# Clustered attention and two feed-forward layers on one core: two heads by plain loads, a gate, and a new order of the first slots

## The chip, the cores and the metric

One Trainium2 chip, one of its cores. The metric is the device time of one execution in microseconds (us). The core's engines are TensorE (PE; PEld is its weight load), VectorE (DVE), ScalarE (ACT), GpSimd (POOL) and SyncE (SP). SP, ACT and POOL can issue DMA transfers; each works through its own instructions in order, and a DMA whose condition is not met holds up what stands behind it on the same engine.

## The reference

Inputs: q, k, v of 2 batches x 8 heads x 768 positions x 64, and 16 centroids of 64 per head. A query may look at a key only if both have the same nearest centroid:

```
q_assign = argmax(q_n . c_n);  k_assign = argmax(k_n . c_n)      # per head, 16 clusters
scores = q @ k^T / 8, and -1e9 where q_assign != k_assign
attn = exp(scores - rowmax) / (rowsum + 1e-9);   o = attn @ v
x = o as [1536, 512]
x = (silu(x @ w_gate) * (x @ w_val)) @ w_out                      # d_ff 1536
p = domain_probs / rowsum                                         # 4 experts
out = sum over e of p[:, e] * (relu(x @ w1[e]) @ w2[e])           # d_ff 1024
```

## The kernel before

Everything runs on one core in two parts, `attention()` and `moe()`. The order of instructions on each engine is the order in which the program writes them. Products use float32r operands in two parts: a high part (the value rounded by a cast) and a low part (the value less its high part).

**Operands of a head.** There are 16 heads g (8 per batch). In memory `qk[b, h]` holds q and k of a head transposed, 128 rows: the 64 features twice, then q|k, then 768 positions. `t1` (128 x 2 x 768) is to hold, for q (index 0), the high part in rows 0 to 63 and the low part in rows 64 to 127, and for k (index 1) the low part in rows 0 to 63 and the high part in rows 64 to 127. `t2` (80 x 2 x 768) holds the high parts in rows 0 to 63 and 16 cluster rows in 64 to 79: one-hot for q, and 0 or -2^60 for k. `load_qk(g)` lets POOL issue casting DMA loads into t1 and t2 and lets SP load the two plain halves that the low parts are made from (`raw`); `rest_qk` (line 211) subtracts, on DVE for heads 0 and 1, on POOL for the others. Each head thus is read twice over from memory, 1.5 MB in all. `load_v` and `rest_v` do the like for v.

**Cluster steps.** `cluster(g)` is a generator that is advanced step by step: six matmuls for q, six for k (line 246), ACT's copy `sc`, DVE's add, maximum, comparison, tie-breaking product and maximum, one-hot `oh` (lines 255 to 264), six transposes to `pt` on TensorE, and the copies of `pt` into t2 (for head 0 one on ACT and one on DVE, lines 273 and 275; for others four half copies on ACT, lines 283 and 285). `pc` and `pt` live in single PSUM banks, `ps_c`, and `ps_v` for some heads.

**Slots.** 96 score tiles n (128 queries x 768 keys; six per head) are worked on in slots. `LEAD` is 5: slot s computes the scores of tile s+5 (S, lines 303 and 304), its negated maximum (M, line 309, DVE) and the exponential of tile s+4 (E, line 321, ACT with its accumulator read), and transposes two blocks of earlier tiles (line 327), casts them (ACT, line 332), makes low parts (DVE, line 346) and multiplies with v (lines 357 to 363). The letters of `ORDER = "ESTLAtVMlvZB"` give the sequence in a slot; A, Z and B run the side work that `at(slot, "a"|"z"|"b")` and `steps` have put there. A table of offsets per head (CL, CL1, CL2) says at which slots, counted from 6g, its cluster steps run; `load_qk(g)` for g > 3 runs at slot 6g-23, `rest_qk` at 6g-22 and 6g-20. The slots from -22 to -6 hold side work only, from -5 to -1 also scores. `warm(n)` issues n matmuls on zeros (line 451) as filler.

**Opening.** SP loads centroids, identity, the halves of head 0, wt and probs; POOL casts heads 0, 1, 2. `consts_setup` normalizes the centroids (DVE, ACT), transposes them on TensorE and writes `cT` in two parts. Then heads 1 to 3 and v are loaded, and `cluster(0)` runs.

**Second part.** `moe()` works through chunks of weights; TensorE multiplies, ACT and DVE finish the tiles and split the next weights (`w_steps`), whose pieces come by SP (`w_load`, two buffers). `probs_setup` makes the expert factors `pn`.

Of the kernel before, what the change touches and what calls it, by code (L numbers as in the profile page):

```python
# [7 lines left out]
F32 = mybir.dt.float32  # L8
# [10 lines left out]
NCL = 16  # L19
NT = B * S  # L20
# [15 lines left out]
def tile_cluster_attention_moe(ctx, tc, qk, vt, cent, consts, wm1, wm2, probs, out):  # L36
# [137 lines left out]
    def attention():  # L174
        with ExitStack() as ax:
# [14 lines left out]
            ops = {}  # L190

            def load_qk(g):
# [7 lines left out]
                if g == 0:  # L200
                    for j in range(2):
                        G.dma_start(out=t1[:, j], in_=src[:, j])
                else:
                    G.dma_start(out=t1, in_=src)
                G.dma_start(out=t2[0:64], in_=src[0:64])
# [21 lines left out]
            oh_t = [clp.tile([128, NQ, 2, 32], BF16, name=f"oh{h}") for h in range(2)]  # L227
            for h in range(2):
                V.memset(oh_t[h], 0.0)

            def cluster(g):
# [5 lines left out]
                ohn = oh[:, :, :, :NCL]  # L237
                pc = (ps_v if g in (1, 2) else ps_c).tile([128, N, 2, NCL], F32, tag="v" if g in (1, 2) else "c", name="pc")
                sc = clp.tile([128, N, NCL], F32, tag="sc", name="sc", bufs=2)
# [32 lines left out]
                if g == 0:  # L272
                    A.copy(out=t2[64:80, 0], in_=pt[0:16])
                    yield
                    V.tensor_scalar(out=t2[64:80, 1], in0=pt[32:48], scalar1=1.0, scalar2=BIG, op0=ALU.subtract, op1=ALU.mult)  # L275
# [168 lines left out]
            zeros = clp.tile([128, 384], BF16, name="zeros")  # L444
            V.memset(zeros, 0.0)

            def warm(n):
# [4 lines left out]

            consts_load(clp, ("cr", "ident"))
            load_qk(0)
            consts_load(clp, ("wt", "pr"))
            setup, rest = consts_setup(clp, ps_c), rest_qk(0, V)
            for gen in (setup, setup, rest):
                next(gen)
            for gen in (setup, rest):
                next(gen, None)  # L460
            load_qk(1)
            load_qk(2)
            load_v(0)
            load_qk(3)
            head, rest = cluster(0), rest_qk(1, V)
            for i, gen in enumerate((head,) * 10 + (rest, head, rest)):
                if i == 2:
                    warm(6)
                next(gen)
                if i == 8:  # L470
                    warm(6)
            for i in range(5):
                at(i - 4, "b", lambda: warm(3))
# [7 lines left out]
            CL1 = ("-10b", "-10z", "-9a", "-9b", "-9b", "-8a", "-8a", "-8b", "-7a", "-7b", "-7b", "-7z", "-7z")  # L481
            CL2 = ("-13z", "-13z", "-12a", "-12b", "-12b", "-12z", "-11a", "-10a", "-9b", "-9b", "-8b", "-7b", "-7z")
            for g in range(NH):
                c = 6 * g
                if g > 3:
                    at(c - 23, "z", lambda g=g: load_qk(g))
                if g > 1:
                    steps(c, ("-22b", "-20b"), lazy(rest_qk, g, G))
                if g:
                    steps(c, {1: CL1, 2: CL2}.get(g, CL), lazy(cluster, g))  # L490
                    at(c - 8, "z", lambda g=g: load_v(g))
                at(c - 4, "z", lambda g=g: rest_v(g))
# [66 lines left out]

    def consts_load(clp, names):  # L560
        src = {"cr": cent.rearrange("h c d -> (h c) d"), "ident": consts[:, 0:128],
               "wt": consts[:, 128:128 + NCL], "pr": probs}
        for n in names:
            ct[n] = ident if n == "ident" else clp.tile(list(src[n].shape), F32, name=n)
            SY.dma_start(out=ct[n], in_=src[n])

    def consts_setup(clp, ps_c):
        for n, w in (("sq", D), ("ss", 1), ("s1", 1), ("s2", 1), ("cn", 2 * D), ("prs", NT // 128)):
            ct[n] = clp.tile([128, w], F32, name=n)
# [18 lines left out]
        A.copy(out=cT[:, :, 0, :], in_=psv)  # L588
        V.tensor_tensor(out=cT[:, :, 1, :], in0=psv, in1=cT[:, :, 0, :].bitcast(F32), op=ALU.subtract)
        V.tensor_copy(out=identb, in_=ident)  # L590
        V.tensor_copy(out=wtie, in_=ct["wt"])
        V.memset(zero1, 0.0)
        A.activation(out=s2, in_=zero1, func=ACTF.Exp)

    def probs_setup():
        pr = ct["pr"]
        prs = ct["prs"].rearrange("p (t o) -> p t o", o=1)
        V.tensor_reduce(out=prs, in_=pr, axis=AX.X, op=ALU.add)
# [4 lines left out]
    def moe():  # L603
# [295 lines left out]
```

## Time and profile before

| | us |
|---|---|
| median of 3 runs | 1090.57 |
| lowest, highest | 1088.77, 1091.58 |
| span of the profiled execution | 1086.7 |
| TensorE busy in it | 1051.0 |
| DVE, ACT, POOL busy | 715.4, 465.0, 180.7 |

The span runs from the first to the last instruction that the profiler recorded; of the profiled execution's own time the profile gives no more than that, and the runs' times lie 2.1 to 4.9 us above it. Attention takes about the first 290 us, the second part the rest. A busy TensorE is not TensorE at its peak: matmuls are pipelined and their ends are modelled. An engine's time of waiting matters only where the engine that bounds the stage waits too.

### The profile page before, as it was taken

What the parts mean: (1) busy time and instruction counts of PE and PEld (TensorE: products, weight loads), DVE (VectorE), ACT (ScalarE), POOL (GpSimd) and SP (SyncE); (2) the same over time, 40 slices, a digit from 0 to 9 for tenths busy, and PEclk for the clock granted to TensorE, in tenths of its full rate; (3) what the DMA queues carried; (4) which work ended last, traced back from release to release, by engine and by line L of the source; (5) the groups of instructions that cost most, each with busy time, mean ns of one, the idle gap of its engine ahead of it and who ended that gap; (6) DMA issues with size and microseconds to landing.
All of it is one profiled execution on the core that took longest, in us unless ns stands there. A gap on an engine that the chain in (4) does not pass through costs nothing.

```text
span 1086.7 us, 13698 instructions
## 1 busy us (share of the span) xinstructions
PE 1051.0 (97%) x5178; PEld 871.6 (80%) x5178; DVE 715.4 (66%) x1243; ACT 465.0 (43%) x930; POOL 180.7 (17%) x182
## 2 busy tenths in 40 slices
PE   4899999999999999999999999999999999999998
PEld 2788778778788888888888888888888888888887
DVE  4799999898566655646658565655555665555564
ACT  1688888889554224414425222233322223333121
POOL 2526664542100000000101111111011111100100
PEclk9899999999999999999999999999999999999999
DMA  9866677551122212211200101111101011110103
GB/s 204 181 149 160 149 188 168 140 116 35 31 87 68 78 49 68 78 59 59 78 20 21 39 20 39 39 39 39 39 20 32 27 39 39 39 40 22 37 1 116
DMA packets 34801, 77.54 MB, mean 71 GB/s; under 512 B 12432, under 2 KB 17008, under 8 KB 34736
## 3 DMA queue, kind: packets, MB, share of 16 engines
q1 hardware_dynamic: 22560, 55.70, 18.3%
q0 software_dynamic: 12176, 20.97, 9.1%
q8 instruction: 40, 0.66, 0.3%
q14 instruction: 25, 0.20, 0.1%
HBM read 69.34 MB, written 3.19 MB: 67 GB/s over the span
## 4 chain that ended last, share of the span: by engine, by line
PE 88%; DVE 7%; DMA 2%; ACT 1%; issue 1%; SPq 0%; ACTq 0%; DVEq 0%
PE pd L834 24%; PE pb L163 17%; PE pa L704 12%; PE pd L801 9%; PE pa L163 9%; PE ps L327 5%; PE ps L303 2%; PE pb L704 2%; PE ps L304 2%; DVE junk L309 2%; DMA raw<-in_qk 2%; DVE lo L346 2%; PE pv L357 2%; PE pv L362 1%; PE pc L246 1%; PE pv L363 1%
## 5 line engine op out<-in xcount | busy, mean ns | idle before, releaser
L841 DVE SCALAR_TENSOR_TENSOR acc<-pd,pn,acc 128x512 f32<-128x512 f32 (+1 forms) x181 | 133.9, 746 | 89.6 <-PE pd L834 89.5
L834 PE MATMUL pd<-wdl,hh 128*128 128x512 f32 (+1 forms) x386 | 149.7, 388 | 0.0
L834 PE MATMUL pd<-wdh,hh 128*128 128x512 f32 (+1 forms) x386 | 149.7, 388 | 0.0
L834 PE MATMUL pd<-wdh,hl 128*128 128x512 f32 (+1 forms) x386 | 149.7, 388 | 0.0
L712 ACT COPY snap<-pa 128x512 f32<-128x512 f32 x48 | 28.2, 588 | 265.2 <-PE pa L704 265.2
L134 POOL TENSOR_TENSOR ws<-wraw 128x256 f32<-128x256 f32 x16 | 12.3, 772 | 671.8 <-DMA wraw<-in_wm 485.4
L163 PE MATMUL pb<-xh,wuh 128*128 128x512 f32 x264 | 102.7, 389 | 0.0
L163 PE MATMUL pb<-xl,wuh 128*128 128x512 f32 x264 | 102.7, 389 | 0.0
L163 PE MATMUL pb<-xh,wul 128*128 128x512 f32 x264 | 102.7, 389 | 0.0
L309 DVE CUSTOM_DVE_ANT_1 junk<-ps,zero 128x768 bf16<-128x768 f32 x96 | 91.0, 948 | 14.1 <-PE ps L304 13.0
L327 PE MATMUL ps<-ident,P 128*128 128x128 f32 x576 | 87.6, 279 | 12.4 <-DVE lo L346 10.2
L321 ACT ACTIVATE P<-ps,nm 128x768 f32<-128x768 f32 x96 | 87.0, 906 | 16.1 <-DVE nm L309 14.5
L327 PEld LDWEIGHTS ps<-ident,P 128*128 128x128 f32 x576 | 67.0, 141 | 26.8 <-DVE lo L346 17.3
L834 PEld LDWEIGHTS pd<-wdl,hh 128*128 128x128 f32 x386 | 72.5, 188 | 15.0
L834 PEld LDWEIGHTS pd<-wdh,hh 128*128 128x128 f32 x386 | 72.5, 188 | 14.9
L834 PEld LDWEIGHTS pd<-wdh,hl 128*128 128x128 f32 x386 | 72.5, 188 | 14.9
L346 DVE TENSOR_TENSOR lo<-ps,hi 128x384 fp32r<-128x384 f32 x128 | 67.5, 550 | 8.4 <-ACT hi L332 8.1
L303 PE MATMUL ps<-t 80*128 80x384 f32 x192 | 70.0, 365 | 1.6 <-DVE t L275 1.1
L304 PE MATMUL ps<-t 128*128 128x384 f32 x192 | 65.7, 342 | 0.0
L211 POOL TENSOR_TENSOR t<-raw,t 64x768 fp32r<-64x768 f32 x28 | 51.3, 1833 | 82.1 <-DMA raw<-in_qk 59.4
L332 ACT CAST hi<-ps 128x384 fp32r<-128x384 f32 x128 | 56.0, 482 | 19.1 <-PE ps L327 18.6
L717 ACT ACTIVATE hh<-sg 128x512 fp32r<-128x512 f32 x48 | 30.3, 632 | 72.3 <-DVE sg L724 72.3
(166 smaller groups left out, 2317.2 us busy)
## 6 DMA issues: line engine op xcount, KB each, us to landing
wraw<-in_wm SPq DMA_DIRECT2D x68, 512.0 KB, 3.8
t<-in_qk POOLq DMA_DIRECT2D x15, 768.0 KB, 5.7
t<-in_qk POOLq DMA_DIRECT2D x18, 384.0 KB, 6.7
raw<-in_qk SPq DMA_DIRECT2D x32, 192.0 KB, 6.5
x<-x SPq DMA_DIRECT2D x21, 192.0 KB, 5.9
R<-rd SPq DMA_DIRECT2D x16, 192.0 KB, 3.3
out<-acc SPq DMA_DIRECT2D x11, 256.0 KB, 2.0
vs<-in_vt POOLq DMA_DIRECT2D x16, 128.0 KB, 3.9
```

Of the source, the lines that this page charges most:

```text
L163: T.matmul(out=ps, lhsT=w[:, o:o + 128], rhs=x, start=(k == 0 and m == 0), stop=(k == 3 and m == 2))
L303: T.matmul(out=ps, lhsT=t2[:, 0, qs], rhs=t2[:, 1, ks], start=True, stop=False)
L304: T.matmul(out=ps, lhsT=t1[:, 0, qs], rhs=t1[:, 1, ks], start=False, stop=True)
L309: V.tensor_tensor_reduce(out=junk.rearrange("p (c n) -> p c n", c=2), in0=S_t[n][:, :, :384], in1=zero1.rearrange("p (o n) -> p o n", o=1) ...
L321: A.activation(out=P_t[n].rearrange("p (c n) -> p c n", c=2), in_=S_t.pop(n)[:, :, :384], func=ACTF.Exp, scale=0.125, bias=nm_t.pop(n), ac ...
L327: T.transpose(ps[:, i * 128:(i + 1) * 128], P_t[3 * u + i][:, j * 128:(j + 1) * 128], ident)
L332: A.copy(out=hi, in_=ps)
L346: V.tensor_tensor(out=lo, in0=ps, in1=hi.bitcast(F32), op=ALU.subtract)
L704: T.matmul(out=ps, lhsT=w[:, o:o + 128], rhs=r, start=first and i == 0 and m == 0, stop=i == 1 and m == 2, skip_group_check=not first)
L801: T.matmul(out=ps, lhsT=w[:, o:o + 128], rhs=x[:, f, sl], start=(n == 0), stop=(n == len(terms) - 1))
L834: T.matmul(out=ps, lhsT=x[:, f, ts_], rhs=w[:, f * DM + cs.start:f * DM + cs.stop], start=(f == 0 and m == 0), stop=(f == FC - 1 and m == 2))
L841: V.scalar_tensor_tensor(out=y, in0=ps, scalar=pe, in1=y, op0=ALU.mult, op1=ALU.add)
```

## The change

- Heads 0 and 1 (`load_raw`): SP loads q and k as they are, both copies of the features, into tiles of the pool of the exponentials (tag "P"). The high parts come by copies on the chip: `hi_raw` into t1 on ACT, `hi_t2` into t2 on DVE for head 0 and on ACT for head 1; `low_raw` subtracts on DVE. The four cast loads and four half loads of these heads are gone.
- Identity and wt are loaded from ACT's queue. `gate`: ACT copies one column of head 0's k into it, POOL overwrites it after; all POOL DMA issues of later heads and of v stand behind that on POOL.
- The opening is written out anew, with fillers of 11, 3, 5 and 8 matmuls, and ends with the first cluster step of head 1. The slots start at -5 instead of -22; head 1's remaining cluster steps run in slots -4 to 0, head 2's in 0 to 5 (`pc` now in `ps_c`), head 3's in 6 to 11, head 4's in 8 to 17. Loads of heads 3 and 4 are issued at slots -3 and 2. Filler triples run in slots -5 to -1 (before -4 to 0).
- Head 0's last operand is made in four halves, three on ACT and one on DVE.
- probs are loaded and `probs_setup` runs in the second part, after the first chunk's up products. The first two weight loads are issued at slot 9 instead of -2. The `zeros` memset stands ahead of those of `oh`, `zero1` is set with them.

```diff
+            def load_raw(g):
+                src = qk[g // H, g % H]
+                raw = [pp.tile([128, S], F32, tag="P", name="rawqk") for _ in range(2)]
...
+                for j in range(2):
+                    SY.dma_start(out=raw[j], in_=src[:, j])
+            def hi_raw(g, j, copy):
+                copy(out=ops[g]["t1"][:, j], in_=ops[g]["raw"][j])
+            def low_raw(g, j):
+                r = slice(64, 128) if j == 0 else slice(0, 64)
+                t = ops[g]["t1"][r, j]
+                V.tensor_tensor(out=t, in0=ops[g]["raw"][j][r], in1=t.bitcast(F32), op=ALU.subtract)
+            def hi_t2(g, j, copy):
+                copy(out=ops[g]["t2"][0:64, j], in_=ops[g]["raw"][j][0:64])
...
-                pc = (ps_v if g in (1, 2) else ps_c).tile([128, N, 2, NCL], F32, ...)
+                pc = (ps_v if g == 1 else ps_c).tile([128, N, 2, NCL], F32, ...)
...
-            consts_load(clp, ("cr", "ident"))
-            load_qk(0)
-            consts_load(clp, ("wt", "pr"))
...
+            consts_load(clp, SY, ("cr",))
+            load_raw(0)
+            consts_load(clp, A, ("ident", "wt"))
+            load_raw(1)
+            setup, head = consts_setup(clp, ps_c), cluster(0)
+            warm(11)
+            next(setup)
+            next(setup)
+            hi_raw(0, 0, A.copy)
+            next(setup)
+            low_raw(0, 0)
+            warm(3)
+            next(head)
+            hi_raw(0, 1, A.copy)
+            A.copy(out=gate, in_=ops[0]["raw"][1][:, 0:1])
+            G.memset(gate, 0.0)
+            low_raw(0, 1)
+            next(head)
+            warm(5)
+            next(setup, None)
+            load_v(0)
+            load_qk(2)
+            for j in range(2):
+                hi_t2(0, j, V.tensor_copy)
+            next(head)
+            for j in range(2):
+                hi_raw(1, j, A.copy)
+            for _ in range(5):
+                next(head)
+            warm(8)
+            low_raw(1, 0)
+            next(head)
+            next(head)
+            low_raw(1, 1)
+            for j in range(2):
+                hi_t2(1, j, A.copy)
+            head = cluster(1)
+            next(head)
...
-                steps(12 * (p + 1), ("1a", "2b", "2z"), recip(p))
+                steps(12 * (p + 1), ("1a", "2z", "2b"), recip(p))
...
+            CL1 = ("-4a", "-4z", "-3a", "-3a", "-3z", "-2a", "-2z", "-1a", "-1z", "-1b", "0z", "0b")
+            CL2 = ("-12z", "-12b", "-11a", "-11z", "-11b", "-10z", "-10b", "-9a", "-9b", "-9b", "-8z", "-7z", "-7b")
+            CL4 = ("-16a", "-16z", "-16b", "-15a", "-15z", "-14a", "-12a", "-9a", "-9b", "-9b", "-8z", "-7z", "-7b")
+            steps(0, CL1, head)
+            LQ = {3: -3, 4: 2}
+            RQ = {2: ("-13z", "-13b"), 3: ("-15b", "-13b"), 4: ("-19b", "-17b")}
...
-            at(-3, "z", probs_setup)
             for _ in range(2):
-                at(-2, "z", w_load)
+                at(9, "z", w_load)
...
-            for slot in range(-22, NS):
+            for slot in range(-LEAD, NS):
```

## Rows read from the trace of the kernel before

**Rows 1.** The page, part 1: busy us (share of the span) xinstructions.
```profile
PE 1051.0 (97%) x5178; PEld 871.6 (80%) x5178; DVE 715.4 (66%) x1243; ACT 465.0 (43%) x930; POOL 180.7 (17%) x182
```

**Rows 2.** Busy us by stage; last columns: granted clock, DMA share, GB/s.
```profile
0.00:24.29 24.29, 8.22 (x31) 4.92 (x32) 8.81 (x27) 4.34 (x7) 6.02 (x14) 1.00 1.17 196
24.29:42.39 18.10, 14.76 (x82) 12.52 (x82) 11.04 (x26) 8.33 (x19) 10.01 (x9) 0.81 1.02 212
42.39:73.66 31.27, 30.58 (x207) 25.68 (x205) 28.79 (x61) 25.54 (x59) 12.84 (x13) 1.00 0.54 117
73.66:277.00 203.34, 192.88 (x1293) 163.79 (x1293) 185.47 (x386) 175.63 (x399) 101.75 (x83) 1.00 0.60 141
277.00:1086.70 809.70, 804.55 (x3574) 664.65 (x3572) 481.27 (x746) 251.19 (x448) 50.09 (x65) 1.00 0.14 45
```

**Rows 3.** TensorE in order of time: start, us, instruction [idle before <-releaser]; line 303.
```profile
24.29 0.45 PE L303 MATMUL ps<-t 80*128 80x384 f32 x1 [1.11 <-DVE t L275]
...
42.39 0.48 PE L303 MATMUL ps<-t 80*128 80x384 f32 x1
...
275.94 0.34 PE L303 MATMUL ps<-t 80*128 80x384 f32 x1
```

**Rows 4.** The chain of waits, opening: start, us, what.
```profile
4.73 19.97 DMA raw<-in_qk
```

**Rows 5.** DVE in order of time, 0 to 32 us.
```profile
8.24 0.96 DVE L211 TENSOR_TENSOR t<-raw,t 64x768 fp32r<-64x768 f32 x1 [3.26 <-DMA raw<-in_qk]
...
15.09 0.17 DVE L591 CAST wtie<-wt 128x16 bf16<-128x16 f32 x1 [5.44 <-DMA wt<-in_consts]
...
18.04 0.36 DVE L255 TENSOR_TENSOR sc<-pc,sc 128x192 f32<-128x192 f32 x1 [1.91 <-ACT sc L253]
...
19.89 0.36 DVE L264 TENSOR_TENSOR oh<-eq,mw 128x192 bf16<-128x192 bf16 x1
...
22.30 0.96 DVE L211 TENSOR_TENSOR t<-raw,t 64x768 fp32r<-64x768 f32 x1 [2.05 <-DMA raw<-in_qk]
...
29.65 0.20 DVE L598 TENSOR_REDUCE prs<-pr 128x12 f32<-128x48 f32 x1
...
31.10 0.43 DVE L601 TENSOR_TENSOR pn<-pr,prs 128x48 f32<-128x48 f32 x1
```

**Rows 6.** The table by stage again, for the first 6 us.
```profile
0.00:4.50 4.50, 0.00 (x0) 0.00 (x0) 2.01 (x11) 1.49 (x2) 3.46 (x10) 1.00 0.51 100
4.50:6.00 1.50, 0.47 (x1) 0.18 (x1) 0.45 (x3) 0.44 (x2) 1.50 (x3) 1.00 1.32 281
```

**Rows 7.** ACT's groups up to 60 us: xcount | busy us, mean ns | idle before.
```profile
L321 ACT ACTIVATE P<-ps,nm 128x768 f32<-128x768 f32 x12 | 10.9, 907 | 11.1 <-DVE nm L309 10.9
L332 ACT CAST hi<-ps 128x384 fp32r<-128x384 f32 x12 | 5.4, 482 | 4.1 <-PE ps L327 4.1
L321 ACT ACTIVATION_READ_ACCUMULATOR P<-ps,nm 128x1 f32 x12 | 2.4, 198 | 0.0
...
L574 ACT ACT_TABLE_LOAD x1 | 1.3, 1283 | 0.7 <-PEq L887 0.7
```

**Rows 8.** TensorE in order of time, 17 to 27 us: fillers and cluster matmuls.
```profile
17.49 2.10 PE L451 MATMUL warm<-zeros 128*128 128x384 bf16 x6
...
25.82 0.73 PE L246 MATMUL pc<-cT,t 128*128 128x32 f32 x6
26.41 0.66 PE L451 MATMUL warm<-zeros 128*128 128x384 bf16 x3
```

**Rows 9.** The table by stage, 34.4 to 38.4 us.
```profile
34.40:38.40 4.00, 3.95 (x20) 3.48 (x21) 0.87 (x2) 3.44 (x8) 3.50 (x3) 0.50 1.01 314
```

**Rows 10.** POOL, then DVE, in order of time, 27 to 47 us.
```profile
27.06 3.71 POOL L211 TENSOR_TENSOR t<-raw,t 64x768 fp32r<-64x768 f32 x2 [15.78 <-DMA raw<-in_qk]
...
45.60 1.82 POOL L211 TENSOR_TENSOR t<-raw,t 64x768 fp32r<-64x768 f32 x1 [2.73 <-issue]
...
45.84 1.80 DVE L264 TENSOR_TENSOR oh<-eq,mw 128x192 bf16<-128x192 bf16 x1
```

More of the change, by code (lines that the diff above doesn't have):

```diff
@@ L190, in attention @@
             ops = {}
+            def load_raw(g):
+                src = qk[g // H, g % H]
+                raw = [pp.tile([128, S], F32, tag="P", name="rawqk") for _ in range(2)]
+                ops[g] = {"t1": qkp.tile([128, 2, S], F32R, tag="t1", name="t1", bufs=4),
+                          "t2": qkp.tile([80, 2, S], F32R, tag="t2", name="t2", bufs=4), "raw": raw}
+                for j in range(2):
[8 more added lines that the diff above has]
+                copy(out=ops[g]["t2"][0:64, j], in_=ops[g]["raw"][j][0:64])
             def load_qk(g):
@@ L199, in load_qk @@
                 SY.dma_start(out=raw[0:64], in_=src[0:64, 1])
[L200 to L204, printed above, removed]
+                G.dma_start(out=t1, in_=src)
                 G.dma_start(out=t2[0:64], in_=src[0:64])
@@ L227, in attention @@
             oh_t = [clp.tile([128, NQ, 2, 32], BF16, name=f"oh{h}") for h in range(2)]
-            for h in range(2):
-                V.memset(oh_t[h], 0.0)
             def cluster(g):
@@ L237, in cluster @@
                 ohn = oh[:, :, :, :NCL]
-                pc = (ps_v if g in (1, 2) else ps_c).tile([128, N, 2, NCL], F32, tag="v" if g in (1, 2) else "c", name="pc")
+                pc = (ps_v if g == 1 else ps_c).tile([128, N, 2, NCL], F32, tag="v" if g == 1 else "c", name="pc")
                 sc = clp.tile([128, N, NCL], F32, tag="sc", name="sc", bufs=2)
@@ L272, in cluster @@
                 if g == 0:
-                    A.copy(out=t2[64:80, 0], in_=pt[0:16])
-                    yield
-                    V.tensor_scalar(out=t2[64:80, 1], in0=pt[32:48], scalar1=1.0, scalar2=BIG, op0=ALU.subtract, op1=ALU.mult)
+                    hs = [slice(i * 384, (i + 1) * 384) for i in range(2)]
+                    A.activation(out=t2[64:80, 1, hs[0]], in_=pt[32:48, hs[0]], func=ACTF.Copy, scale=BIG, bias=-BIG)
+                    V.tensor_scalar(out=t2[64:80, 1, hs[1]], in0=pt[32:48, hs[1]], scalar1=1.0, scalar2=BIG, op0=ALU.subtract, op1=ALU.mult)
+                    for i in range(2):
+                        A.copy(out=t2[64:80, 0, hs[i]], in_=pt[0:16, hs[i]])
                     yield
@@ L445, in attention @@
             V.memset(zeros, 0.0)
+            for h in range(2):
+                V.memset(oh_t[h], 0.0)
+            V.memset(zero1, 0.0)
             def warm(n):
@@ L451, in warm @@
                     T.matmul(out=ps, lhsT=zeros[:, 0:128], rhs=zeros, start=True, stop=True)
-            consts_load(clp, ("cr", "ident"))
-            load_qk(0)
-            consts_load(clp, ("wt", "pr"))
[L456 to L461, printed above, removed]
-            load_qk(2)
[L463 to L471, printed above, removed]
+            gate = clp.tile([128, 1], F32, name="gate")
+            consts_load(clp, SY, ("cr",))
[19 more added lines that the diff above has]
+            load_v(0)
+            load_qk(2)
+            for j in range(2):
[14 more added lines that the diff above has]
+            next(head)
             for i in range(5):
-                at(i - 4, "b", lambda: warm(3))
+                at(i - 5, "b", lambda: warm(3))
             for i in range(4):
@@ L563, in consts_load @@
         for n in names:
-            ct[n] = ident if n == "ident" else clp.tile(list(src[n].shape), F32, name=n)
-            SY.dma_start(out=ct[n], in_=src[n])
+            ct[n] = ident if n == "ident" else pool.tile(list(src[n].shape), F32, name=n)
+            eng.dma_start(out=ct[n], in_=src[n])
     def consts_setup(clp, ps_c):
-        for n, w in (("sq", D), ("ss", 1), ("s1", 1), ("s2", 1), ("cn", 2 * D), ("prs", NT // 128)):
+        for n, w in (("sq", D), ("ss", 1), ("s1", 1), ("s2", 1), ("cn", 2 * D)):
             ct[n] = clp.tile([128, w], F32, name=n)
@@ L589, in consts_setup, with probs_setup @@
         V.tensor_tensor(out=cT[:, :, 1, :], in0=psv, in1=cT[:, :, 0, :].bitcast(F32), op=ALU.subtract)
+        yield
         V.tensor_copy(out=identb, in_=ident)
         V.tensor_copy(out=wtie, in_=ct["wt"])
-        V.memset(zero1, 0.0)
         A.activation(out=s2, in_=zero1, func=ACTF.Exp)
-    def probs_setup():
-        pr = ct["pr"]
-        prs = ct["prs"].rearrange("p (t o) -> p t o", o=1)
+    def probs_setup(pr, prs_t):
+        prs = prs_t.rearrange("p (t o) -> p t o", o=1)
         V.tensor_reduce(out=prs, in_=pr, axis=AX.X, op=ALU.add)
@@ L612, in moe @@
         acc2 = acc.rearrange("p (t n) -> p t n", n=DM)
+        consts_load(ap_, SY, ("pr",))
+        prs = ap_.tile([128, NT // 128], F32, name="prs")
         side = {"work": iter(()), "x": iter(()), "steps": 0, "calls": 0}
@@ L852, in moe @@
                 up(k)
+                if i == 0:
+                    probs_setup(ct["pr"], prs)
                 if k[1] % 2:
```

12 lines of the change are left out of this document (5 added, 7 removed).

## The prediction

> **What bounds the kernel now.** I read the page's busy line first: TensorE works in 97% of 1086.7 us [rows 1], so time can be won only where it stands idle or slow. The table by stage says where: up to 24.29 us it works 8.22 us, from there to 42.39 us 14.76 of 18.10 at a mean clock of 0.81, then 30.58 of 31.27, 192.88 of 203.34, and 804.55 of the last 809.70 [rows 2]. I name the steps of the attention part by their score matmuls of line 303: S0 opens slot -5 at 24.29, S6 (the first of head 1) opens slot 1 at 42.39, S95 comes at 275.94 [rows 3]: from S6 on a slot takes (275.94-42.39)/89 = 2.62 us. The change touches what lies ahead of S6 and the slots just after it, so the question is when S6 comes.
>
> The chain of waits shows the opening as one DMA wait of 19.97 us for halves of q and k ("raw") [rows 4]. The DVE timeline has the single waits behind it: the first subtract of line 211 starts at 8.24 after 3.26 us without its half; the cast of wt waits 5.44 us for a small load that stood behind others, and as DVE works in order, head 0's second subtract comes only after it, at 15.2; the first subtract of head 1 waits 2.05 us more, to 22.30 [rows 5], and head 0's last operand, line 275, stands behind that on DVE; S0 waits for it [rows 3].
>
> Own time against the median: of the profiled execution the page gives the span, 1086.7 us; the three runs lie 2.1 to 4.9 us above that, their median 3.9. What moves S6 moves both, so I subtract from both.
>
> **Head 0's data.** Before, the DMA engines carry head 0's halves and cast loads mixed with those of heads 1 and 2. They moved 0.45 MB in the first 4.5 us (100 GB/s) and 0.42 MB in the next 1.5 (281 GB/s) [rows 6]. After, SP's queue holds the centroids (0.03 MB), then q and k of head 0 (0.39 MB each), then head 1; identity and wt (0.07 MB) go by ACT's queue, and POOL's cast loads stand behind the gate. At the old pace the first operand is complete when 0.49 MB have come, at 4.7, the second at 0.89 MB, at 6.1; I take 4.8 and 6.3, and 7.9 and 9.5 for head 1. Bounds for the second: 5.5, if 281 GB/s hold from 2.7 us on; 8.2, if it lands no sooner than the half that freed DVE at 8.24 [rows 5].
>
> **Head 0's chain to S0.** Copies from SBUF on ACT and DVE are new. ACT's 128x768 lies between 0.91 (line 321, as many columns) and 0.96 (two casts of 384); I take 0.91. DVE's 64x768 lies between a half and the whole of the 0.95 of line 211; I take 0.95, the nearest row [rows 5, 7].
> ACT: first copy 4.8 to 5.7, cT 0.3 to 6.0, second copy 6.3 to 7.2, gate, table load of 1.28 [rows 7] and exp to 8.9. DVE: the rest of cT to 6.3, two subtracts to 8.2, two small casts to 8.6, two copies to 10.5. TensorE: twelve cluster matmuls from 7.3 to 9.3 (0.73 us for six at 26 us, up to twice that at half the clock [rows 8]). ACT's sc copy to 9.7. DVE's seven steps from add to one-hot took 18.04 to 20.25, 2.2 us [rows 5]: 10.5 to 12.7. In TensorE's order 13 fillers stand ahead of the transposes: 2.9 us at 0.22 or 4.6 at 0.35, the two rates of line 451 [rows 8], to 12.2 or 13.9. Transposes under 1 us, then three half copies of 0.48 on ACT [rows 7] (the fourth, on DVE, beside them). S0: 14.7 to 16.3, taken as 15.2, 9.1 us earlier. With the operands at their bounds: 14.4 to 17.5.
>
> **S0 to S6.** Before, 18.1 us. TensorE runs at granted 0.50 (the 1.2 GHz level) from 34.4 to 38.4 [rows 9], after an idle stretch that was head 1's chain: its raw, then the four steps of probs_setup, from 29.65 to 31.53 on DVE, ahead of head 1's add [rows 5]. Probs_setup now runs in the second part, beside TensorE at 99% and DVE at 59% [rows 2]: nothing there, 1.9 us if that cover were gone. What is late next is ACT: two copies for head 1 1.8, five exp with their accumulator read 5.5, sc 0.3, four half copies 1.9, two transposed casts of slot 0 1.0 [rows 7]: 10.5 us. S0 itself, the first max and the joints between ACT and DVE come on top; I take 12 to the last half copy. Then the twelve cluster matmuls of head 2, put at slot 0 ahead of S6 and in the PSUM bank that head 1's half copies free last: 1.5 us [rows 8], of which I count 1.2. S6 = 15.2 + 13.2 = 28.4 instead of 42.39: 14.0 earlier. Bounds of this stretch 11 and 16 us: S6 at 25.4 to 33.5.
>
> **DVE beside POOL.** Head 2's two POOL subtracts fall at about 18 to 23 us, beside head 1's DVE steps. At 45.84 a one-hot step took 1.80 us beside a POOL subtract begun at 45.60; undisturbed it took 0.36 [rows 5, 10]. Bounds: 0 to 2 x 1.5 us. I take 0, since between those DVE steps stand maxima that read PSUM and ACT is the later engine. The Trainium skill, "SBUF — State Buffer", section "Who interferes with whom", speaks against the change here: a DVE instruction with two SBUF inputs and a POOL instruction that reads SBUF shut each other out for a whole instruction. The row agrees; by the rule the time would be 3 us later, 1080.
>
> **After S6.** Heads 3 and 4 begin their cluster steps later and end by the slots that need them, so slots 0 to 5 hold less DVE work and slots 6 to 17 more; from S6 on there are six cluster matmuls more than before, 0.6 us. The weight loads at slot 9 have three slots, 7.9 us, to land; if they didn't, ACT would stand for the rest, under 2 us. "2b" and "2z" only change places in a list (z runs before b in each slot): nothing. The memsets only change places. The load of probs waits on SP for memory of the first part; behind it stand weight loads, covered by two pieces in flight; at most 2 us.
>
> **Sum:** -14.0 + 0.6 = -13.4: span 1073.3, median 1077.2; I say 1077.
>
> **Rivals.** (A) Smaller gain, 1084: the DMA engines are shared more than I count (only POOL is gated; SP sends v and raw of heads 2 and 3 without a wait), S0 comes 2 us later, and slots -5 to -1 run at the 1.2 GHz level, where four score matmuls and three fillers take 2.4 us instead of 1.4: 5 us more. 1077 + 7 = 1084. For it: the clock fell in this very stretch [rows 9]. Against it: fillers stand in every gap.
> (B) Larger gain, 1072: S0 at 14.4 and ACT packed without a joint bring S6 at 25.4, 17 us gained; freer slots 0 to 5 give 1.5 more. For it: DVE is busy 28.79 of 31.27 us in those slots [rows 2]. Against it: the steps come back in slots 6 to 17.
> (C) Not faster: head 2 is late. Its cast loads start behind the gate and v, at about 9 us instead of 4, and TensorE, in order, stands at slot 0 ahead of its matmuls; all that follows waits. Before, POOL's subtracts for head 2 began at 27.06, after 15.78 us of waiting [rows 10], 23 us after the issue. Another 23 us make it 32, two subtracts of 1.85 36, S6 37.5: still 5 us gained, 1085.6. From 28 us of loading on nothing is gained; at 33 us the time is 1095.6, with heads 3 and 4 queued behind. Against it: by then 3.9 MB have to come, and at the 196 GB/s of the first stage [rows 2] that is 20 us; heads 0 and 1 no longer load everything twice.
> (D) No difference, 1090: S6 comes early, and slots 1 to 12 give it all back because heads 3 and 4 come late in turn. It needs 13 us of new waits; each of these heads has over 10 us from issue to use.
>
> **Chances:** forecast (1074 to 1081) 0.58; A with C's mild form 0.20; B 0.12; D 0.04; C 0.06. The range, 1070.5 to 1084.5, leaves out C, D and the far end of A. Under 0.3% (3.3 us, about what a measurement of this kernel can tell from no change) falls D: faster 0.90, same 0.04, slower 0.06.
>
> **What would show it.** After the change: ACT's two copies for head 0 near 4.8 and 6.3 (the loads), no DVE wait for wt, S0 at 14 to 17, S6 at 25 to 33 (ACT the later engine between), no stretch at the lower clock after S0 (else A), POOL's first subtract for head 2 begun before 23 us (else C), and S6 to S95 233 to 236 us (before 233.6; else D). Wrong would be S6 after 34, or S6 early and S95 not.

## The result, and the profile after

The changed kernel takes 1080.36 us (median of 6 runs, 1077.92 to 1083.08), the kernel before, run beside it, 1089.67 (6 runs, 1087.5 to 1095.86). The ratio is 0.9909, 95% interval 0.988 to 0.9937: the medians lie 9.31 us apart. The profiled execution of the changed kernel took 1080.05 us, its span is 1078.3 (before 1086.7), so the two profiles differ by 8.4 us. Line numbers moved: the score matmuls are now lines 318 and 319, the exponential 336, the casts of transposed blocks 347, the one-hot 277, POOL's subtract 226.

The page's busy line of TensorE answers to [rows 1], the table by stage to [rows 2]: stage and its length, then busy us of PE, PEld, DVE, ACT, POOL; granted clock, DMA share, GB/s. The cuts stand at S0, S6, S18 and S95.

```profile
PE 1054.8 (98%) x5193; PEld 873.3 (81%) x5193; DVE 717.7 (67%) x1245; ACT 470.2 (44%) x939; POOL 178.1 (17%) x178
```

```profile
0.00:15.09 15.09, 11.28 (x52) 6.36 (x53) 9.88 (x30) 7.66 (x14) 4.67 (x12) 0.89 1.03 262
15.09:27.98 12.89, 10.53 (x70) 8.26 (x70) 9.01 (x21) 10.49 (x22) 8.22 (x8) 1.00 0.94 215
27.98:62.03 34.05, 32.40 (x213) 27.95 (x212) 28.45 (x61) 24.99 (x58) 13.71 (x13) 0.95 0.50 115
62.03:267.19 205.16, 194.96 (x1286) 165.08 (x1285) 187.88 (x385) 174.90 (x398) 101.08 (x83) 0.98 0.60 140
267.19:1078.30 811.11, 805.64 (x3580) 665.67 (x3579) 482.45 (x751) 252.15 (x450) 50.38 (x66) 1.00 0.14 45
```

TensorE in order of time, line 318, the counterparts of [rows 3]: S0, S6 and S95.

```profile
15.09 0.44 PE L318 MATMUL ps<-t 80*128 80x384 f32 x1 [0.88 <-ACT t L290]
...
27.98 0.42 PE L318 MATMUL ps<-t 80*128 80x384 f32 x1
...
267.19 0.34 PE L318 MATMUL ps<-t 80*128 80x384 f32 x1
```

The reader is to subtract three times. S0 is 9.20 us earlier, S6 14.41, S95 only 8.75. So 5.66 us are given back between S6 and S95 (239.21 us instead of 233.55), and after S95 nothing changes (811.1 and 810.8). The clock column shows where: 0.95 and 0.98 in the two stages after S6, 1.00 in both before. (Before, the lower clock lay between S0 and S6, 0.81 in [rows 2]; the 0.89 of the first stage here lies in the fillers ahead of S0.)

The opening went as forecast. ACT, then DVE, in order of time; the second copy finds its data, and wt is there at once (before: 5.44 us [rows 5]).

```profile
5.00 0.83 ACT L201 CAST t<-rawqk 128x768 fp32r<-128x768 f32 x1 [1.50 <-DMA rawqk<-in_qk]
...
5.98 0.83 ACT L201 CAST t<-rawqk 128x768 fp32r<-128x768 f32 x1
6.72 0.19 ACT L486 COPY gate<-rawqk 128x1 f32<-128x1 f32 x1
```

```profile
6.35 1.94 DVE L206 TENSOR_TENSOR t<-rawqk,t 64x768 fp32r<-64x768 f32 x2
...
8.35 0.19 DVE L633 CAST wtie<-wt 128x16 bf16<-128x16 f32 x1
8.46 0.98 DVE L209 CAST t<-rawqk 64x768 fp32r<-64x768 f32 x2
...
11.66 0.36 DVE L277 TENSOR_TENSOR oh<-eq,mw 128x192 bf16<-128x192 bf16 x1
```

The 5.66 us can be split by the rows. TensorE's idle time from S6 to S95 is 1.65 + 10.20 = 11.85 us (the stages above, length less busy). Before it was 0.69 + 10.46 = 11.15 [rows 2]: 0.7 us more. The rest is the clock. From S6 to S95 the granted clock is 1.00 outside three stretches. In these it falls to 0.50, the 1.2 GHz level; by the table by stage:

```profile
28.00:33.00 5.00, 5.00 (x27) 4.87 (x26) 3.19 (x7) 2.00 (x6) 3.74 (x3) 0.66 1.31 222
83.00:88.00 5.00, 4.93 (x24) 4.11 (x25) 3.76 (x11) 2.16 (x5) 2.03 (x3) 0.66 0.68 100
148.00:153.00 5.00, 5.00 (x26) 4.86 (x26) 4.81 (x8) 3.02 (x9) 4.37 (x3) 0.66 0.47 151
```

A mean of 0.66 over 5 us is 3.4 us at half speed (2 x 0.34 x 5), 10.2 us in the three. TensorE is busy nearly throughout, so about half of it is lost: 5.1 us. With the 0.7 us of idle time that is 5.8 for the 5.66. Each stretch follows waits of TensorE. The first wait is that of head 2's cluster matmuls, ahead of S6, for the PSUM bank that ACT's half copies free last (they end at 26.5; the profile names no releaser, and e_halves_early below moves these copies); the later ones are for low parts that DVE makes late. TensorE in order of time:

```profile
26.64 1.48 PE L259 MATMUL pc<-cT,t 128*128 128x32 f32 x12 [1.89 <-issue]
...
83.07 0.55 PE L342 MATMUL ps<-ident,P 128*128 128x128 f32 x3 [0.90 <-DVE lo L361]
...
148.00 0.55 PE L342 MATMUL ps<-ident,P 128*128 128x128 f32 x3 [1.49 <-DVE lo L361]
...
190.23 1.01 PE L342 MATMUL ps<-ident,P 128*128 128x128 f32 x6 [1.87 <-DVE lo L361]
```

A wait alone is not enough: the 1.87 us before 190.23 bring no fall (granted 1.00 from 184 to 194), nor do the longest ones in the kernel before from S6 on, 1.51 us before 132.55 and 1.47 before 157.29.

DVE is late where its two-input steps in SBUF meet POOL's subtract. The place where most was lost at full clock is S14 to S15, 4.52 us instead of 2.59; POOL, then DVE, in order of time:

```profile
48.66 2.05 POOL L226 TENSOR_TENSOR t<-raw,t 64x768 fp32r<-64x768 f32 x1 [3.12 <-issue]
...
51.52 1.80 POOL L226 TENSOR_TENSOR t<-raw,t 64x768 fp32r<-64x768 f32 x1
```

```profile
49.06 1.77 DVE L274 TENSOR_TENSOR eq<-eq,wtie 128x192 bf16<-128x192 bf16 x1
...
51.60 1.94 DVE L277 TENSOR_TENSOR oh<-eq,mw 128x192 bf16<-128x192 bf16 x1
```

The one-hot of 0.36 us (at 11.66) takes 1.94 beside a POOL subtract: it ends 0.2 us after POOL does.

### The profile page after: what moved, and what is told of

Its sections match the earlier page's. It is cut to its first block, busy times and chain, and to the rows that moved or that the text cites. A ratio compares the mean times of both kernels' runs of the same rounds, so it can differ in the third digit from the quotient of the medians.

```text
span 1078.3 us, 13732 instructions
## 1 busy us (share of the span) xinstructions
PE 1054.8 (98%) x5193; PEld 873.3 (81%) x5193; DVE 717.7 (67%) x1245; ACT 470.2 (44%) x939; POOL 178.1 (17%) x178
## 4 chain that ended last, share of the span: by engine, by line
PE 91%; DVE 7%; ACT 1%; issue 1%; DMA 0%; SPq 0%; ACTq 0%; DVEq 0%
PE pd L876 24%; PE pb L163 17%; PE pa L746 12%; PE pd L843 9%; PE pa L163 9%; PE ps L342 5%; PE ps L318 2%; PE ps L319 2%; PE pb L746 2%; DVE junk L324 2%; PE pv L372 2%; PE pv L377 2%; PE pv L378 2%; DVE lo L361 2%; PE pc L259 2%; PE pu L163 1%
## 5 line engine op out<-in xcount | busy, mean ns | idle before, releaser
L324 DVE CUSTOM_DVE_ANT_1 junk<-ps,zero 128x768 bf16<-128x768 f32 x96 | 91.1, 949 | 14.7 <-PE ps L319 13.8
L342 PE MATMUL ps<-ident,P 128*128 128x128 f32 x576 | 88.4, 281 | 12.2 <-DVE lo L361 11.2
```

What stands on the lines that cost most here:

```text
L324: V.tensor_tensor_reduce(out=junk.rearrange("p (c n) -> p c n", c=2), in0=S_t[n][:, :, :384], in1=zero1.rearrange("p (o n) -> p o n", o=1) ...
L342: T.transpose(ps[:, i * 128:(i + 1) * 128], P_t[3 * u + i][:, j * 128:(j + 1) * 128], ident)
```

## Experiments

All runs in one table. S0, S6 and S95 are starts in the profiled execution; "half" is the time at the 1.2 GHz level between S6 and S95, worked out as above, 2 x (1 - granted clock) x length, with the stretches cut at S6 and S95; "idle" is TensorE's idle time there. The ratio is to the kernel before on the same chip.

| kernel | S0 | S6 | S95 | half | idle | median us | ratio, 95% interval |
|---|---|---|---|---|---|---|---|
| before | 24.3 | 42.4 | 275.9 | 0 | 11.2 | 1089.67 | 1 |
| after | 15.1 | 28.0 | 267.2 | 10.2 | 11.9 | 1080.36 | 0.9909 [0.988, 0.9937] |
| e_cast_loads | 15.9 | 32.4 | 271.4 | 11.8 | 11.5 | 1084.15 | 0.9961 [0.9932, 0.9991] |
| e_no_gate | 16.5 | 30.2 | 269.4 | 8.5 | 12.1 | 1081.87 | 0.9929 [0.99, 0.9957] |
| e_wt_behind | 16.3 | 32.4 | 269.5 | 8.9 | 11.1 | 1082.47 | 0.9941 [0.9913, 0.9969] |
| e_before_wt | 20.0 | 39.3 | 274.6 | 4.1 | 11.4 | 1086.19 | 0.9981 [0.995, 1.0012] |
| n_before | 21.6 | 39.6 | 267.8 | 0 | 6.8 | 1079.64 | 0.9888 [0.9863, 0.9912] |
| n_after | 16.1 | 29.5 | 260.3 | 9.2 | 6.4 | 1075.46 | 0.9855 [0.9829, 0.9881] |
| e_halves_early | 14.7 | 25.8 | 268.4 | 10.2 | 15.6 | 1081.09 | 0.9899 [0.9879, 0.9919] |
| e_fill | 14.8 | 28.4 | 265.0 | 6.8 | 11.0 | 1080.40 | 0.9896 [0.9868, 0.9925] |
| e_split | 14.7 | 28.9 | 265.4 | 11.7 | 10.2 | 1079.13 | 0.9901 [0.9863, 0.9939] |
| e_split_before | 20.3 | 38.2 | 276.0 | 12.9 | 11.4 | 1089.02 | 0.9987 [0.9961, 1.0012] |
| e_split_early | 16.4 | 30.0 | 264.7 | 6.8 | 11.3 | 1075.97 | 0.9867 [0.983, 0.9904] |
| e_sub_early | 15.1 | 28.9 | 261.7 | 3.4 | 10.1 | 1074.04 | 0.9847 [0.9814, 0.9881] |

In every row S95 - S6 less idle less half of "half" is 219.7 to 222.8 us, the work itself: idle time and clock account for the length of the stage to within 1.6 us either way. Each row is one profiled execution.

### Which part brings S6 forward

**e_cast_loads**: after, but heads 0 and 1 by cast loads and half loads as before; loads behind the gate otherwise the same.

```diff
+                SY.dma_start(out=raw[64:128], in_=src[64:128, 0])
+                SY.dma_start(out=raw[0:64], in_=src[0:64, 1])
                 for j in range(2):
-                    SY.dma_start(out=raw[j], in_=src[:, j])
+                    G.dma_start(out=t1[:, j], in_=src[:, j])
+                G.dma_start(out=t2[0:64], in_=src[0:64])
...
-                copy(out=ops[g]["t1"][:, j], in_=ops[g]["raw"][j])
+                pass
...
-                copy(out=ops[g]["t2"][0:64, j], in_=ops[g]["raw"][j][0:64])
+                pass
...
```

> The changed kernel with heads 0 and 1 loaded as before (four halves by SP, casts by POOL, no copies on the chip), everything else as changed. Theory (the doubled loads cost the opening its time): head 0 and 1 need 3.1 MB again instead of 1.6, at 0.2 to 0.26 MB/us, so head 0's last operand comes at 9 to 12 us instead of 6.0 and S0 at 19 to 23 instead of 15.1; S6 at 31 to 36; time 1083 to 1088. Rival (the order and the early wt made the gain, the loads hardly matter): S0 at 15 to 17, time within 2 us of the changed kernel, 1080 to 1082.

S0 came only 0.8 us later (the theory had 4 to 8), S6 4.4; the time is 3.8 us longer, 1084.15. Head 0's second operand came 1.9 us later, at 7.91 instead of 5.98, but the copies on the chip fall away. From S0 to S6 no instruction of TensorE, DVE or ACT waits for a load of head 1 by the profile; what is longer is slots -4 to -1, where TensorE runs at the 1.2 GHz level. ACT in order of time, the table by stage, and TensorE in order of time (the wait ahead of S6, 1.89 us in the changed kernel):

```profile
7.91 0.19 ACT L490 COPY gate<-t 128x1 f32<-128x1 f32 x1 [2.09 <-DMA t<-in_qk]
```

```profile
15.00:25.00 10.00, 9.12 (x37) 7.42 (x37) 6.46 (x14) 4.04 (x9) 6.20 (x6) 0.66 1.25 308
```

```profile
30.16 2.38 PE L263 MATMUL pc<-cT,t 128*128 128x32 f32 x12 [1.83 <-POOL vs L244]
```

**e_no_gate**: after, without the copy into `gate` and POOL's memset on it; POOL's loads start at once.

```diff
-            A.copy(out=gate, in_=ops[0]["raw"][1][:, 0:1])
-            G.memset(gate, 0.0)
```

> The changed kernel without the gate, so POOL issues the cast loads of v and head 2 from the start. Theory (loads share the DMA engines): 1.3 MB of POOL's run beside head 0's 0.9, head 0's second operand comes at 8 to 9.5 us instead of 6.0, S0 at 16.5 to 18.5; 1 to 3 us of it arrive at S6; time 1081 to 1083.5. Rival (SP's queue keeps its own pace, the gate does nothing): S0 at 15 to 15.5, time as changed within 1 us.

S0 is 1.4 and S6 2.3 us later, the time 1081.87. Head 0's second copy starts at 6.23, not at 8 to 9.5 as the theory had it; a load comes late for head 1 alone. But ACT is done with head 1's copy at 13.90 and then waits 1.01 us for TensorE's transposes, which stand behind fillers that took 4.34 us (3.72 in the changed kernel), more of them at the 1.2 GHz level. So the wait for head 1 did not set S0. ACT, then TensorE, in order of time:

```profile
6.23 0.83 ACT L201 CAST t<-rawqk 128x768 fp32r<-128x768 f32 x1
...
13.07 0.83 ACT L201 CAST t<-rawqk 128x768 fp32r<-128x768 f32 x1 [2.07 <-DMA rawqk<-in_qk]
14.92 0.48 ACT L287 ACTIVATE t<-pt 16x384 fp32r<-16x384 bf16 x1 [1.01 <-PE pt L283]
```

```profile
9.76 4.34 PE L469 MATMUL warm<-zeros 128*128 128x384 bf16 x13
14.03 0.85 PE L283 MATMUL pt<-identb,oh 128*64 128x128 bf16 x6
```

**e_wt_behind**: after, with identity and wt on SP's queue, wt behind heads 0 and 1.

```diff
-            consts_load(clp, SY, ("cr",))
+            consts_load(clp, SY, ("cr", "ident"))
             load_raw(0)
-            consts_load(clp, A, ("ident", "wt"))
             load_raw(1)
+            consts_load(clp, SY, ("wt",))
```

> The changed kernel with identity on SP's queue ahead of head 0 and wt on it behind head 1. Theory (a small load waits for all that stands ahead of it on its queue): wt lands behind 1.7 MB, at 9 to 11 us; DVE, in order, waits for it 1 to 2.5 us ahead of head 0's copies and add; S0 at 15.5 to 17.5, S6 later by 0.5 to 2; time 1080.5 to 1082.5. Rival (ACT's fillers on TensorE and ACT's copies are the later chain): S0 within 0.4 us of 15.1, no change.

DVE waits 0.69 us for wt and S0 is 1.2 us later. But in slots -4 to -1 TensorE then runs at the 1.2 GHz level (a score matmul takes 0.52 instead of 0.34), and S6 is 4.4 us later, where the theory had 0.5 to 2; the time is 1082.47. DVE in order of time:

```profile
9.09 0.17 DVE L633 CAST wtie<-wt 128x16 bf16<-128x16 f32 x1 [0.69 <-DMA wt<-in_consts]
```

**e_before_wt**: the kernel before, with wt loaded ahead of head 0 and `probs_setup` moved to slot 30.

```diff
-            consts_load(clp, ("cr", "ident"))
+            consts_load(clp, ("cr", "ident", "wt"))
...
-            at(-3, "z", probs_setup)
+            at(30, "z", probs_setup)
```

> The kernel before with two edits alone: wt is loaded ahead of head 0's halves, and probs_setup runs at slot 30 instead of -3. Theory (the loads of head 1 end the opening next): the wait of 5.4 us for wt goes, but line 275 stays behind head 1's subtract, whose half comes at 22 us, so S0 stays at 23 to 24.5; only the 1.9 us of probs_setup are won ahead of S6: 1087 to 1089. Rival (wt held the opening): S0 at 18.5 to 20, time 1084 or less.

S0 20.0, S6 39.3, the time 1086.19: not told apart from before, as the interval holds 1. S0 lies where the rival had it, but so does that of e_split_before, 20.3, which has the old opening (see below). So the two small moves alone are no substitute for the new opening.

Undone one by one, loads, gate and wt cost 4.4, 2.3 and 4.4 us at S6 and 3.8, 1.5 and 2.1 in the median; of these times only that of the loads stands out, and its interval still overlaps that of the changed kernel. These S6 are no clean prices of the three parts. Seven executions with the opening of the changed kernel (after, n_after, e_halves_early, e_fill, e_split, e_split_early, e_sub_early) have S0 at 14.7 to 16.4, so that of 15.9, 16.3 and 16.5 cannot be told from theirs. Two of the seven, e_split_early and e_sub_early, also run slots -4 to -1 at the 1.2 GHz level, and their S6 is 4.2 and 3.1 us behind that of e_halves_early, with plain loads, gate and early wt all in place; they differ from it only in POOL's pieces. That the opening as a whole brings S6 forward is clear (38.2 to 42.4 before, 25.8 to 30.0 in the seven); which part brings how much is not shown.

### Where 5.7 us are given back

**n_before, n_after**: POOL's subtract cut to one column, so the low parts of q and k of heads 2 to 15 are left out; everything else as before and after.

```diff
-                    t = t1[r, i]
-                    eng.tensor_tensor(out=t, in0=raw[r], in1=t.bitcast(F32), op=ALU.subtract)
+                    t, x = t1[r, i], raw[r]
+                    if eng is G:
+                        t, x = t[:, 0:1], x[:, 0:1]
+                    eng.tensor_tensor(out=t, in0=x, in1=t.bitcast(F32), op=ALU.subtract)
```

> The kernel before, with POOL's subtract for heads 2 to 15 cut to one of 768 columns; the low parts of these heads are left out, nothing else. Theory (DVE and POOL shut each other out, and the early start put more of DVE's steps beside POOL's subtracts): DVE steps beside a POOL subtract fall back to their usual time; S6 to S95 shrinks from 233.6 to 224 to 230. Rival (the give-back is something else): it stays above 231.

> The changed kernel with the same cut: POOL's subtract for heads 2 to 15 on one of 768 columns, low parts left out. Theory (DVE and POOL): S6 to S95, 239.2 as changed, comes within 1.5 us of the same cut in the kernel before; the time then lies 13 to 15 us below that one. Rival (other work, or the lower clock after the idle stretch at slot 0): S6 to S95 stays 4 to 6 us longer than in the cut kernel before, and the two times lie 8 to 10 us apart.

With POOL short, S6 to S95 falls to 228.2 and 230.8 us, by 5.3 and 8.4, and from S12 on the two are equal (213.23 and 213.28; with the subtract 217.75 and 222.86). So in these profiles, one each, that part of the difference goes with POOL's subtracts, though n_after still has one fall of the clock there. The 2.5 us that remain lie between S6 and S12, where TensorE stands at the 1.2 GHz level from 28 to 35 us in n_after. But the two are 7.2 us apart in span and 4.2 in the median, not the 13 to 15 expected: S6 differs by 10.1 here instead of 14.4, since n_before's opening, the same code as before's, came 2.7 us earlier in its profile (see below). The medians speak against the theory: with the subtracts cut, the change is worth 4.2 us (4 executions each), less than the 9.3 with them and not more.

**e_halves_early**: head 1's last half copies at slot -1 instead of 0, so that S6's cluster matmuls find their bank free.

```diff
-            CL1 = ("-4a", "-4z", "-3a", "-3a", "-3z", "-2a", "-2z", "-1a", "-1z", "-1b", "0z", "0b")
+            CL1 = ("-4a", "-4z", "-3a", "-3a", "-3z", "-2a", "-2z", "-1a", "-1z", "-1z", "-1b", "-1b")
```

> The changed kernel with head 1's last two half copies at slot -1 instead of 0, so head 2's cluster matmuls, which wait for their bank, need not wait for slot 0's casts on ACT. Theory (this wait and the half clock after it are part of the give-back): TensorE's idle stretch of 1.89 us at slot 0 shrinks below 0.7, no stretch at the lower clock follows, S6 at 26 to 26.7 instead of 27.98 and S8 2.5 to 3.5 us earlier; time 1077 to 1078.5. Rival (exp of tile 4, now behind the halves, is late in its turn): S6 earlier but S8 not by more than 1 us; time 1079.5 to 1081.

S6 came 2.2 us earlier, S8 3.3, as the theory had it, and the time did not move: 1081.09. S8 to S9 then took 5.23 us, and S10 was no earlier than after the change; POOL, then DVE, in order of time:

```profile
29.99 1.82 POOL L226 TENSOR_TENSOR t<-raw,t 64x768 fp32r<-64x768 f32 x1 [0.41 <-DMA t<-in_qk]
```

```profile
30.09 1.94 DVE L272 TENSOR_TENSOR eq<-sc,mx 128x192 bf16<-128x192 f32 x1
```

An earlier slot met POOL's next subtract; TensorE then stood 1.59 us before 33.23 and fell to the 1.2 GHz level behind it, and the gain was gone.

**e_fill**: after, with 8 filler matmuls at slot 0, in the idle time before S6.

```diff
+            def fill():
+                ps = ps_v.tile([128, 384], F32, tag="v", name="fill")
+                for _ in range(8):
+                    T.matmul(out=ps, lhsT=zeros[:, 0:128], rhs=zeros, start=True, stop=True)
+
+            at(0, "z", fill)
```

> The changed kernel with eight fillers at slot 0 ahead of head 2's cluster matmuls, in the bank of pv. Theory (the clock falls after the idle 1.89 us and costs on its own): the fillers fill 1.4 us of it, S6 stays at 28.0 within 0.3, the granted clock from 28 to 33 us is 0.95 or more instead of 0.66, and S8 comes 1 to 1.7 us earlier; time 1078.5 to 1079.5. Rival (the chain between ACT and DVE sets these slots, not the clock): S8 within 0.5 us of 33.75, no change in time.

The first stretch at the lower clock is gone, by the table by stage:

```profile
28.00:33.00 5.00, 4.74 (x34) 4.44 (x34) 3.53 (x9) 2.53 (x8) 4.23 (x3) 1.00 1.30 240
```

In this execution the fall went with the idle time before it. S6 is 0.5 us later, S8 0.6 earlier (the theory had 1 to 1.7), S95 2.2 earlier. The median, 1080.40, shows nothing of it. Two stretches remained, at 143 to 149 and 184 to 190.

**e_split, e_split_before**: POOL's subtracts and row-scaling steps in four pieces each, so that DVE's short steps wait for a quarter only.

```diff
-                    eng.tensor_tensor(out=t, in0=raw[r], in1=t.bitcast(F32), op=ALU.subtract)
+                    k = 4 if eng is G else 1
+                    for x in range(k):
+                        cs = slice(x * S // k, (x + 1) * S // k)
+                        eng.tensor_tensor(out=t[:, cs], in0=raw[r, cs], in1=t[:, cs].bitcast(F32), op=ALU.subtract)
...
-                eng.tensor_tensor(out=xu, in0=xu, in1=R, op=ALU.mult)
+                parts(eng, lambda c: eng.tensor_tensor(out=xu[:, c], in0=xu[:, c], in1=R[:, c], op=ALU.mult))
...
```

> The changed kernel with POOL's subtracts for heads 2 to 15, and its three steps of the row scaling, each cut into four instructions of 192 columns. Theory (a DVE step that meets a POOL instruction waits for its end, up to 1.5 us; TensorE then stands idle, and the clock falls for 3.4 us at a time): a DVE step waits for a quarter at most, 0.3 to 0.5 us; the sum of such waits falls from 27.6 us to 6 to 14, TensorE's idle time from S6 to S95 from 11.9 to 6 to 9, stretches at the lower clock from three to none or one; S6 to S95 228 to 233 instead of 239.2, time 1070 to 1075. Rival (POOL comes back at once with the next quarter and DVE waits as long in all; POOL's own four fixed costs add 0.5 us a half and heads come late): the sum stays above 20, time 1079 to 1083.

> The kernel before with the same quarters. Theory (the give-back of the change is clock stretches set off by such waits): S6 to S95, 233.6, falls to 226 to 230, the same as in the changed kernel with quarters within 2 us; the time falls to 1083 to 1087, so the change as such is worth 12 to 14.5 us with quarters on both sides. Rival (before had no clock stretches after S6 for a reason of its own): the two S6 to S95 lie 4 us or more apart, and the change stays worth 8 to 10.

The steps on DVE did become short: the one-hot's mean fell from 935 to 398 ns, the comparison's from 1026 to 427 (14 each). DVE's groups from 28 to 270 us, the one-hot after the change, then in e_split:

```profile
L277 DVE TENSOR_TENSOR oh<-eq,mw 128x192 bf16<-128x192 bf16 x14 | 13.1, 935 | 0.0
```

```profile
L280 DVE TENSOR_TENSOR oh<-eq,mw 128x192 bf16<-128x192 bf16 x14 | 5.6, 398 | 0.0
```

The time did not follow: 1079.13, and 1089.02 for the kernel before with the same edit, so the change is worth 9.9 us with quarters on both sides, not 12 to 14.5. The theory that the exclusion is what costs the 5.7 us falls in this form. Idle fell by 1.6 us; half clock is 11.7 us instead of 10.2, and in the kernel before it rose from 0 to 12.9.

**e_split_early**: quarters and early halves together.

> The same quarters, and head 1's last two half copies at slot -1. Theory: with the long waits gone, the 2.2 us that the early halves brought to S6 (25.8 instead of 28.0) and the clock that stayed up behind it arrive at the end: 2 to 3.5 us below the quarters alone, 1067 to 1072. Rival (what is won at S6 is given back in the slots after it whatever POOL does): within 1 us of the quarters alone.

S95 came 2.5 us earlier than after the change, though S6 was 2.0 later; 1075.97 us. That is 3.2 us below the quarters alone, as the theory had it, and each of the six executions lies below each of the six of e_split. But it is not for the theory's reason, as S6 came 1.1 us later than in e_split, and 1067 to 1072 was missed.

**e_sub_early**: the subtract in quarters, the row-scaling whole, early halves.

> After the change, with POOL's subtracts of line 226 cut in four and head 1's last half copies one slot earlier, as in the kernel that has quarters and early halves; but the row-scaling steps of POOL (sum, product, subtract) stay whole. In the kernel with all of them in quarters, DVE's integer step for the v weights took 3.17 us (0.42 after the change) beside the quarters of a product, and S37 to S39 took 10.9 us instead of 6.2, with TensorE at the 1.2 GHz level behind it. If these quarters are what sets off that stretch, S37 to S39 takes 6 to 7 us, no half clock falls at 112 to 120 us, S95 comes at 258 to 262 instead of 264.7, and the time is 1071 to 1074 us. Rival: whichever DVE step meets a POOL step next pays, and one stretch at the lower clock takes the place of another: S95 stays at 263 to 267 and the time at 1075 to 1079 us.

1074.04 us, the lowest median here. S95 came at 261.7, in the theory's range, but not for its reason: S37 to S39 still took 9.6 us with the row-scaling whole, and the stretch behind it is the only one left after S6. POOL, DVE and TensorE in order of time:

```profile
109.97 1.83 POOL L435 TENSOR_TENSOR x<-x,R 128x768 f32<-128x768 f32 x1
```

```profile
109.41 2.69 DVE L114 TENSOR_SCALAR wb<-wraw 128x512 int32<-128x512 int32 x1
```

```profile
113.48 0.55 PE L345 MATMUL ps<-ident,P 128*128 128x128 f32 x3 [2.52 <-DVE lo L364]
```

DVE's step on the weights takes 0.42 us when POOL is idle (at 113.91 after the change); here 2.69. With the row-scaling in quarters it took 3.17 (e_split_early) and 2.98 (e_split): what differs from the changed kernel is when the step falls, rather than how POOL's work is cut. Against the changed kernel itself this version was not timed side by side; the two intervals, 0.9814 to 0.9881 and 0.988 to 0.9937, just touch.

### What stays open

Which wait makes the clock fall is not settled: 1.87 us at 190 us did not, 1.49 at 148 did, and e_split_before shows three stretches in code that differs from before's only in POOL's pieces. Where the stretches lie is known for one execution of each kernel alone.

How much of the lower clock an execution has in all is on record for every timed one, as the mean granted clock beside its span. By 2 x (1 - clock) x span, 65 executions of the kernel before, timed beside the experiments, have 0 to 28 us of it (clock 1.00 to 0.987), on average 14.1 (standard error 0.7); its profiled execution had about 8 (0.996). Six of the changed kernel have 11 to 22 us, on average 16.2 (1.5), the profiled one about 15 (0.993). So on average the change adds some 2 us at the 1.2 GHz level, 1 us of time, and not the 5.1 us that the two profiles show from S6 to S95: the profile of before had little of the lower clock. With half of that time taken off every span (an estimate; over the 65 executions a us at the lower clock goes with 0.3 us of span), the means are 1081.1 before and 1070.8 after, 10.3 apart. By the same estimate e_cast_loads, e_no_gate and e_wt_behind come to 1071.7, 1071.0 and 1070.7, with 20.8, 16.8 and 19.9 us at the lower clock: much of what undoing a part cost in the median is clock.

## Why the prediction came out as it did

**Head 0.** Forecast S0 15.2, measured 15.09, step by step: copies at 5.00 and 5.98 (4.8 and 6.3), sc copy by 9.78 (9.7), one-hot by 12.02 (12.7), transposes by 13.43. One term was off: DVE's copies of 64x768 took 0.49 each, about the lower bound, not 0.95.

**S0 to S6.** Forecast 13.2 us with ACT as the later engine, measured 12.89. ACT's last half copy ended at 26.54, 11.45 us after S0 (12 forecast), with ACT busy 9.49 of them: the counted items were about 1 us shorter than the 10.5. (ACT's 10.49 up to S6 agrees by chance: it holds a sixth exp that the sum had not.) Then came the cluster matmuls and S6, as worked out, 1.44 us (1.2). The sum up to S6, -14.0, was -14.41 by the two profiles.

**That profile of before was late.** Two other executions with the same opening (n_before, e_split_before; only POOL's subtracts of head 2 differ ahead of S6) have S0 at 21.6 and 20.3 and S6 at 39.6 and 38.2; with [rows 3] the means are 22.1 and 40.1. Four with the whole changed opening (after, n_after, e_fill, e_split) lie at 28.0 to 29.5, mean 28.7. So the gain at S6 is rather 11.4 us, three less than the one pair of profiles shows, and the sum over it 11.4 - 0.6 = 10.8, against 9.3 between the medians. That the forecast -14.0 met -14.41 was thus in part luck: it was counted from a late S6, and the changed kernel was set against the same one. The forecast median, 1077, was 3.4 us low: 13.4 us were to be won and 9.3 were; 2.3 of the difference is this late start (42.4 against 40.1), about 1 the clock (below). By the same token e_before_wt's S6 of 39.3 is 0.7 us ahead of before, not 3.1.

**After S6: the mis-sized term.** The prediction set 0.6 us, "six cluster matmuls more", and expected no stretch at the lower clock after S0. Measured: 5.66 us, of which about 5 are three stretches at 1.2 GHz and 0.7 idle time. In the two profiles this is what turns the 14.4 us into 8.4. Over all timed executions the lower clock costs the change about 1 us instead of 5 (above), and 10.8 less this is near the 9.3 measured. The prediction read the fall of the clock in [rows 9] as the price of head 1's idle chain, and took it to go with that chain. It did not go for good: one fall followed the wait before S6 (e_fill, which fills that wait, has none there), and two followed waits in slots 20 and 44. Of rival A the fall of the clock came, but elsewhere: slots -5 to -1 ran at 1.00 in this profile. In e_split_early and e_sub_early they had 6.8 us at the 1.2 GHz level, where rival A had put them.

**DVE beside POOL** was weighed at 0 to 3 us and taken as 0. Head 2's subtracts ran at 15.49 to 19.21 and did no harm. But the wait returned wherever heads 3 and later have their steps: at S14 to S15 it took 1.9 us. The Trainium skill, "SBUF — State Buffer", section "Who interferes with whom", gives the rule for whole instructions; the traces agree (0.36 to 1.94 us beside 1.80), and the n pair shows that without the subtract the stage is 5.3 to 8.4 us shorter in both kernels. It was a cost that the kernel had already; that the change added to it is not shown.

**The other rivals.** (C) POOL began head 2's subtracts at 15.49, not after 23: no late head. That the plain loads of heads 0 and 1 left room for it is likely but not shown apart. (D) is excluded by S95. (B): ACT did not pack without joints (busy 9.49 of the 11.45 us), and S6 to S95 did not get shorter.

## What to carry to other kernels

Take the start from more than one profiled execution where an opening rests on DMA waits: three of the same code lay 4 us apart, against 9.3 us for the whole change. When idle time is removed from the front, count what the idle does next, stretch by stretch: engine waits that cost nothing by themselves can be followed by microseconds at half clock, so compare granted clock and idle time of every stage, not only the busy line. Before a fall of the clock is called a price of the change, look at the mean granted clock of all timed executions: here the one profile of before had about 8 us of the lower clock where the average is 14. A step moved earlier meets the other engines' work at a new phase; e_halves_early gained 2.2 us at S6 and had lost all of it 13 us later, at S10, to a subtract that it had missed before and a fall of the clock behind that wait.

## What the runs showed of the hardware

- Three falls of the granted clock to 0.50, 3.4 us each, from S6 to S95 after the change, where the profile of before had none; score matmuls then start 0.32 us apart instead of 0.17.
- A DVE step with one input was long beside POOL too: the integer step took 2.69 us instead of 0.42 beside a product on POOL of 1.83. Cutting POOL's step in four helped the two-input steps (935 to 398 ns).
- Opening: S0 of the same code at 24.3, 21.6 and 20.3 us before, at 14.7 to 16.4 in seven executions with the changed one.
- The mean granted clock of 65 executions of one kernel ran from 0.987 to 1.00.
- A load of 8 KB behind head 0 and head 1 on SP's queue held DVE for 0.69 us (e_wt_behind). Before, behind head 0's two halves on SP's queue and beside POOL's cast loads, it was 5.44 [rows 5].
